# Weights to 32 bits by other operations on three engines, xn on ScalarE, and wider tiles in eight steps

## Chip, cores and metric

The kernel runs on one core of one Trainium2 chip. The time is that of the device, in microseconds (us), for one execution of the whole program. TensorE is called PE, VectorE DVE, ScalarE ACT, GpSimd POOL; SP is the engine whose queue issues the loads and stores.

## The reference

Two parts follow one another. The first is a gated recurrence over 768 steps for 4 batches and 8 heads of 40 (q, k, v, an input gate, a forget gate, an output gate). The second is a normalisation of the 320 columns with a weight g_ln, a layer of 1,280 with a cut at zero, and a second matrix back to 320, added to the input.

```python
for t in range(S):
    m_new = np.maximum(f_gate[:, :, t] + m, i_gate[:, :, t])
    f_stab, i_stab = np.exp(f_gate[:, :, t] + m - m_new), np.exp(i_gate[:, :, t] - m_new)
    C = f_stab * C + i_stab * einsum('bhd,bhe->bhde', vt, kt)
    n = f_stab * n + i_stab * kt
    y[:, :, t] = sigmoid(o_gate[:, :, t]) * (C @ qt) / np.maximum(np.abs(n @ qt), 1.0)
x = y.transpose(0, 2, 1, 3).reshape(B, S, 320)
xn = (x - mu) / np.sqrt(var + 1e-06) * g_ln
out = x + np.maximum(xn @ w_ch1, 0.0) @ w_ch2
```

The two weight matrices arrive as 64-bit floats.

## The kernel before

The 768 steps are cut into 6 chunks of 128, so with 4 batches there are 24 tiles, numbered `st` (chunk 0 is tiles 0 to 3). Two tiles make a pair `p`, and the dense layers run on pairs, 12 of them.

A tile of the recurrence is computed in chunk form. The gates give a table `w` of decay factors, made by a load of a row to all partitions (`G`, line 204), an affine select on POOL (`sel`, line 312) and exponentials on ACT (`ex`, line 323); for tiles 0 to 3 PE makes the argument instead (`gx`, lines 332 and 338). `S` (line 355) is k times q per head, in matmuls of 40 rows whose stationary side has 128 columns for tiles 0 to 3 and two times 64 after that. `P` (line 362) multiplies it by `w` on DVE. `int` (line 391) multiplies the carried state by the scaled q (`qm`, line 368, POOL, with the loaded tile `eg`), again in two halves of 64 columns, and `pv` (line 440) adds the part within the chunk. `kv` (line 406), `sd` and `st` carry the state on. `n1`, `n2` and `n3` (lines 453 to 477) divide, apply the output gate and take the sum of each row on DVE; the last two instructions of `n3` scale that sum to minus the mean (line 475) and write `xn = (y - mean) * g` (line 477). `sq` (line 484) squares and sums on ACT, `np` (lines 490 and 491) makes the inverse deviation `rs` on POOL.

For the dense layers PE transposes xn (`T`, lines 502 and 503); `xh` (ACT, line 509) rounds the result to the matmul's 32-bit format and `xl` (DVE, lines 517 and 520) keeps the residue. `m1` (line 536) does the first matrix in 8 matmuls for each block of 128 of the 1,280 columns: high weight by high x, low by high, high by low. `hh` (ACT, line 541) and `hl` (DVE, line 548) cut at zero and split again; `m2` (lines 563 to 565) does the second matrix in three matmuls per block, `ob` (line 570) adds it to y, scaled by `rs`, and `out` stores it.

The weights come in eleven pieces called keys: 0 is the last 64 rows of the first matrix, the odd keys are 512 columns of its first 256 rows, the even ones 640 columns of the second matrix. A key is loaded as 64-bit words (`wl`, line 587). `cA` (ACT, line 596) takes the absolute value of the high words, `cX` (DVE, line 603) cuts it from below, `cT` (DVE, lines 609, 613 and 617) shifts and masks in three steps, the last writing over the low words. `cH` (ACT, line 638) rounds the result to the high part, `cL` (POOL, line 644) subtracts it and leaves the low part. `cR` copies the pieces of key 0 to the other half of the partitions.

`ORDER` is one list of words written out ahead of the run; a word calls the function of that name, and each engine executes its own instructions in the list's order. Every load and store is issued by SP in that order too, and waits there for its data or its buffer. `fill` (line 681) is a matmul into a bank that nobody reads; 22 of them stand among the first words. The first m1 of the list is that of pair 0, when keys 3, 2, 0 and 1 have been converted. Keys 4 to 10 follow among the dense layers of pairs 0 and 1.

Of the kernel before, what the change touches and what calls it, by code (L numbers as in the profile page):

```python
# [46 lines left out]
gm.3 st.1 st.0 ex.3.1 S.2@4@6 tok.1 P.0.0 cL.1 P.0.1 gta.2@0 cR.0 gtr.1@5 gr.2 gca.2 P.2.1 pv.0 gg.3 n3.1 ld.5 S.3@0@1
cR.2 fill.512 P.2.0 sq.1 sel.5 gtr.2@6 gate.3 fill.513 P.3.1 gex.3 gst.3 gu.3 ex.5.0 gse.3 fill.512 gcr.2 n1.0
fill.512 P.3.0 fill.512 G.4 ex.5.1 n2.0 int.2@0@1 np.1 gta.3@4 ld.4 fill.512 gm.4 int.3@2@3 fill.512 gr.3 gca.3 gg.4
gcr.1 n3.0 gtr.3@6 pv.3 sig.1 pv.2 gcr.3 km.2 sq.0 gate.4 n1.3 gst.4 gex.4 km.3 T.0@4 n2.3 eg.2 T.1@5 n1.2 kv.2@6 gu.4  # L50
xh.0 n2.2 gse.4 xh.1 xl.0 kv.3@2 st.2 S.5@0@3 xl.1 st.3 np.0 gta.4@1 gm.5 sel.4 m1.0.0.0@6 wl.4 gr.4 P.5.0 n3.2
m1.0.0.1 gg.5 ex.4.0 S.4@2@4 wl.5 ex.4.1 P.5.1 gtr.4@5 gca.4 n3.3 hh.0.0 m1.0.1.0@0 qm.5 wl.7 sq.2 T.2@3 m1.0.1.1 qm.4
hl.0.0 sq.3 P.4.0 xh.2 T.3@1 hh.0.1 m2.0.0.1@6 gate.5 np.2 xh.3 gcr.4 gst.5 xl.2 cA.4 m2.0.0.0@7 cR.1 np.3 xl.3 tok.2
gex.5 gu.5 int.4@2@3 gse.5 cX.4 cA.5 cR.3 m1.1.0.0@5 cT.4.0 ld.6 hl.0.1 m1.1.0.1 cT.4.1 m1.1.1.0@1 sd.4 hh.1.0 cT.4.2
m1.1.1.1 hl.1.0 cH.4 P.4.1 gta.5@0 cA.7 m2.1.0.1@5 cL.4 cX.5 hh.1.1 gca.5 cX.7 m2.1.0.0@4 cT.5.0 wl.9 hl.1.1 m2.0.1.1
wl.6 cT.5.1 sig.2 km.4 m2.1.1.1 cT.7.0 km.5 cT.5.2 m2.0.1.0 cT.7.1 cH.5 pv.4 cT.7.2 cL.5 kv.4@0 cH.7 n1.4 m2.1.1.0
# [5 lines left out]
n2.5 ex.6.1 qm.7 n3.5 m2.0.3.0 m2.1.4.1 km.6 ob.1.0 sq.5 kv.6@0 out.1.0 ob.1.1 np.5 S.6@2@3 out.1.1 tok.4 S.8@4@5
P.6.1 P.6.0 m2.0.4.0 T.5@3 ob.0.0 m2.0.3.1 xh.5 out.0.0 xl.5 m2.0.4.1 m1.2.1.0@2 ob.0.1 G.8 m1.2.1.1 out.0.1 G.9
m1.2.4.0@7 ld.9 sig.4 km.9 ld.11 hh.2.1 km.8 m1.2.0.0@3 hl.2.1 m1.2.0.1 m1.2.2.0@6 sel.8 hh.2.0 ld.10 hl.2.0 m1.2.2.1
ex.8.1 eg.4 m1.2.4.1 ex.8.0 P.8.1 sel.9 m2.2.0.0@2 hh.2.2 P.8.0 m2.2.1.0 G.7 hh.2.4 hl.2.2 ex.9.0 m2.2.0.1@3 hl.2.4
ex.9.1 int.6@4@5 pv.6 sd.6 st.6 S.9@6@7 n1.6 n2.6 m1.2.3.0@0 n3.6 m1.2.3.1 qm.9 P.9.1 sq.6 m2.2.1.1 P.9.0 np.6
m2.2.2.1 hh.2.3 sel.7 hl.2.3 S.11@4@5 ex.7.0 S.7@6@7 m2.2.2.0 ex.7.1 P.7.0 T.6@0 m2.2.3.0 P.7.1 xh.6 xl.6 int.7@6@7
pv.7 sd.7 qm.8 st.7 kv.8@0 n1.7 m2.2.3.1 n2.7 n3.7 m2.2.4.1 int.8@6@7 ob.2.1 sq.7 T.7@1 sd.8 pv.8 out.2.1 st.8 np.7
xh.7 G.12 kv.9@3 xl.7 m2.2.4.0 n1.8 n2.8 m1.3.1.0@0 ob.2.0 n3.8 out.2.0 m1.3.3.0@1 m1.3.1.1 ld.15 sq.8 ld.12 T.8@6
sel.12 G.11 hh.3.1 m1.3.3.1 tok.5 xh.8 hl.3.1 np.8 ex.12.0 m1.3.0.0@7 xl.8 m1.3.2.0@2 ex.12.1 m1.3.0.1 hh.3.3 hl.3.3  # L70
S.10@0@6 hh.3.0 hl.3.0 m1.3.2.1 m2.3.0.0@1 hh.3.2 sel.11 hl.3.2 m1.3.4.0@7 G.10 ex.11.0 m1.3.4.1 m2.3.0.1@2 ex.11.1
P.11.0 eg.5 m2.3.1.0 ld.13 P.11.1 sig.5 km.10 m2.3.1.1 km.11 m2.3.2.1 hh.3.4 hl.3.4 int.9@4@5 sel.10 pv.9 sd.9 st.9
ex.10.0 kv.11@7 n1.9 m2.3.2.0 qm.11 n2.9 G.15 ex.10.1 n3.9 m2.3.3.1 qm.10 m2.3.4.1 ld.16 P.10.1 sq.9 T.9@3 P.10.0
m2.3.3.0 G.13 np.9 xh.9 ob.3.1 m2.3.4.0 xl.9 out.3.1 tok.6 sel.15 m1.4.0.0@4 ob.3.0 out.3.0 m1.4.0.1 ex.15.1 S.12@5@6
ex.15.0 S.13@0@2 hh.4.0 P.12.0 sel.13 P.12.1 kv.10@3 m1.4.2.0@1 hl.4.0 ld.14 ex.13.0 eg.6 m1.4.1.0@5 ex.13.1 P.13.0
m1.4.2.1 P.13.1 m1.4.1.1 hh.4.2 sig.6 km.13 hl.4.2 m2.4.0.1@6 hh.4.1 km.12 m1.4.3.0@4 hl.4.1 m1.4.3.1 m2.4.1.1 hh.4.3
# [5 lines left out]
ex.14.1 m2.4.4.1 P.14.0 tok.7 ex.16.0 m1.5.4.0@2 ob.4.1 P.14.1 out.4.1 m1.5.2.1 ex.16.1 eg.7 m1.5.4.1 hh.5.2 hl.5.2
m2.5.0.0@7 m2.5.0.1@4 m2.4.4.0 m2.5.1.0 ob.4.0 hh.5.4 km.15 sig.7 out.4.0 hl.5.4 m1.5.3.1 km.14 T.13@6 hh.5.3 m2.5.1.1
xh.13 qm.14 hl.5.3 kv.15@5 xl.13 S.16@0@1 qm.15 m2.5.2.0 P.16.1 ld.18 P.16.0 m1.6.1.0@2 m1.6.1.1 ld.17 m2.5.3.0 hh.6.1
hl.6.1 m2.5.4.0 m2.5.2.1 ob.5.0 out.5.0 m2.5.3.1 G.17 int.15@0@1 kv.14@3 sd.15 eg.8 pv.15 st.15 m2.5.4.1 n1.15 n2.15
m1.6.3.0@6 n3.15 int.14@0@1 sel.17 m1.6.0.0@2 ob.5.1 sq.15 sd.14 out.5.1 st.14 np.15 ex.17.0 m1.6.0.1 ld.21 qm.16
ex.17.1 m1.6.2.0@7 qm.17 hh.6.0 m1.6.2.1 tok.8 hl.6.0 m1.6.3.1 hh.6.2 ld.19 hl.6.2 m1.6.4.0@5 hh.6.3 hl.6.3 m2.6.0.1@4
m2.6.0.0@3 m2.6.1.0 m2.6.2.0 m2.6.1.1 sig.8 km.17 km.16 m2.6.2.1 G.18 m2.6.3.1 pv.14 kv.16@2 n1.14 m2.6.3.0 n2.14
n3.14 m1.6.4.1 sel.18 int.16@6@7 hh.6.4 S.18@0@1 sq.14 sd.16 hl.6.4 ex.18.0 np.14 pv.16 st.16 kv.17@5 ex.18.1 n1.16
T.14@2 P.18.0 m2.6.4.0 xh.14 n2.16 P.18.1 m2.6.4.1 xl.14 T.15@0 int.17@6@7 ob.6.0 xh.15 S.17@1@2 ob.6.1 out.6.0 xl.15  # L90
G.21 S.21@3@4 out.6.1 sd.17 eg.9 n3.16 m1.7.2.0@0 ld.20 m1.7.2.1 P.17.1 sq.16 eg.10 P.17.0 m1.7.3.0@2 np.16 hh.7.2
# [654 lines left out]
```

## Time and profile before

| what | value |
|---|---|
| median of 3 runs | 350.67 us (350.58 to 353.99) |
| profiled execution | 352.78 us, its span 351.0 us |
| mean granted clock of PE | 0.966 of full |
| moved by DMA | 49.37 MB, mean 141 GB/s |

The profile is of one execution. The span runs from its first to its last recorded instruction; the execution's own time lies a little above it. Busy time of an engine counts its instructions, not its waiting for others. A row of a group gives the line of the kernel, the engine, the operation, the tiles written and read, the shapes and the count, and, behind the bar, the time that the engine was idle ahead of those instructions and what ended it.

### The profile page before, as it was taken

How to read it: one execution, taken by the hardware profiler on the slowest of the kernel's cores; microseconds unless marked ns; L12 is line 12 of the kernel's file. 1: busy time of each engine (PE TensorE's matmuls, PEld its weight loads, DVE VectorE, ACT ScalarE, POOL GpSimd, SP SyncE). 2: the span in 40 equal slices, each digit the busy share in tenths (PEclk: the TensorE clock that was granted, in tenths of full speed). 3: DMA queues.
4: the chain of work that ended last, by engine and by line, in shares of the span. 5: the costliest groups of instructions: out<-in, count | busy, mean ns of one | idle time of the engine just before them, and what ended most of it. 6: DMA issues, size and time to landing. Idle time of an engine off the chain costs nothing.

```text
span 351.0 us, 11943 instructions
## 1 busy us (share of the span) xinstructions
PE 329.6 (94%) x5189; PEld 305.2 (87%) x5189; DVE 208.5 (59%) x486; ACT 145.5 (41%) x374; POOL 116.1 (33%) x158
## 2 busy tenths in 40 slices
PE   7979999997999699899989989999979999999996
PEld 3558688996899699799989979989979999999995
DVE  6775999998636373864955444286454353383232
ACT  3963673454354336562227214145612932142020
POOL 4476683437421531622322224114331201210000
PEclk9965899999999999999999998999998999999999
DMA  8858379890487059692502358029305803010001
GB/s 235 296 145 216 125 243 251 238 311 12 156 228 185 3 150 304 159 291 47 205 36 67 118 152 266 5 103 254 115 4 169 325 2 88 4 39 1 21 19 40
DMA packets 15953, 49.37 MB, mean 141 GB/s; under 512 B 1916, under 2 KB 5532, under 8 KB 15900
## 3 DMA queue, kind: packets, MB, share of 16 engines
q1 hardware_dynamic: 15900, 48.60, 46.3%
q8 instruction: 41, 0.67, 0.8%
q14 instruction: 12, 0.10, 0.1%
HBM read 43.84 MB, written 4.10 MB: 137 GB/s over the span
## 4 chain that ended last, share of the span: by engine, by line
PE 72%; DVE 16%; issue 4%; DMA 4%; ACT 1%; SPq 1%; POOL 1%; DVEq 0%; POOLq 0%
PE banks L536 25%; PE banks L563 9%; PE banks L565 8%; PE banks L564 8%; PE banks L355 6%; PE banks L440 5%; DMA eg<-esc 3%; PE banks L391 3%; DVE wt L613 3%; DVE wraw L617 2%; PE banks L406 2%; PE banks L338 1%; PE banks L681 1%; PE banks L502 1%; DVE wt L603 1%
## 5 line engine op out<-in xcount | busy, mean ns | idle before, releaser
L563 PE MATMUL banks<-w2h,hh 128*128 128x320 f32 x240 | 77.5, 323 | 0.1
L565 PE MATMUL banks<-w2h,hl 128*128 128x320 f32 x240 | 74.9, 312 | 2.1 <-DVE hl L548 1.3
L564 PE MATMUL banks<-w2l,hh 128*128 128x320 f32 x240 | 74.9, 312 | 1.0 <-issue 1.0
L548 DVE SCALAR_TENSOR_TENSOR hl<-banks,hh 128x512 fp32r<-128x512 f32 x60 | 41.1, 689 | 56.0 <-ACT hh L541 55.8
L541 ACT ACTIVATE hh<-banks 128x512 fp32r<-128x512 f32 x60 | 35.5, 595 | 83.4 <-PE banks L536 76.4
L536 PE MATMUL banks<-xh,w1h 128*128 128x256 f32 x360 | 64.8, 289 | 0.0
L536 PE MATMUL banks<-xh,w1l 128*128 128x256 f32 x360 | 63.1, 285 | 0.0
L323 ACT ACTIVATE w<-w,ar_sb 128x128 f32<-128x128 f32 x160 | 48.7, 389 | 14.6 <-POOL w L312 14.5
L536 PEld LDWEIGHTS banks<-xh,w1h 128*128 128x128 f32 x360 | 52.9, 192 | 0.8 <-issue 0.3
L536 PEld LDWEIGHTS banks<-xh,w1l 128*128 128x128 f32 x360 | 51.9, 191 | 0.0
L536 PE MATMUL banks<-xl,w1h 128*128 128x256 f32 x240 | 48.7, 285 | 0.1
L565 PEld LDWEIGHTS banks<-w2h,hl 128*128 128x128 f32 x240 | 45.5, 190 | 2.8 <-DVE hl L548 1.6
L563 PEld LDWEIGHTS banks<-w2h,hh 128*128 128x128 f32 x240 | 45.5, 190 | 2.6 <-issue 1.6
L362 DVE TENSOR_TENSOR w<-banks,w 128x512 f32<-128x512 f32 x48 | 32.2, 686 | 25.2 <-ACT w L323 14.3
L564 PEld LDWEIGHTS banks<-w2l,hh 128*128 128x128 f32 x240 | 45.6, 190 | 0.4 <-POOL w2l L644 0.4
L368 POOL TENSOR_TENSOR qe<-qk,eg 104x512 f32<-104x512 f32 x20 | 26.8, 1354 | 43.6 <-DMA eg<-esc 29.2
L536 PEld LDWEIGHTS banks<-xl,w1h 128*128 128x128 f32 x240 | 37.3, 191 | 0.3 <-issue 0.3
L312 POOL TENSOR_SCALAR_AFFINE_SELECT w<-w 128x1024 f32<-128x1024 f32 x20 | 21.9, 1097 | 46.6 <-DMA w<-gsc 34.2
L484 ACT ACTIVATE junk<-y,sum 128x320 bf16<-128x320 f32 x24 | 13.4, 560 | 50.6 <-DVE sum L475 50.6
L355 PE MATMUL banks<-qk 40*64 40x128 f32 (+1 forms) x704 | 28.2, 285 | 0.0
L355 PEld LDWEIGHTS banks<-qk 40*64 40x64 f32 (+1 forms) x704 | 23.5, 147 | 2.4 <-issue 0.8
L490 POOL TENSOR_SCALAR rs<-rs 128x1 f32<-128x1 f32 x24 | 5.1, 211 | 53.0 <-ACT junk L484 52.0
(85 smaller groups left out, 421.0 us busy)
## 6 DMA issues: line engine op xcount, KB each, us to landing
tok<-in_tok_dram SPq DMA_DIRECT2D x12, 968.0 KB
w<-gsc SPq DMA_DIRECT2D x20, 512.0 KB
qk<-in_qk_dram SPq DMA_DIRECT2D x24, 416.0 KB
out_dram<-y SPq DMA_DIRECT2D x24, 160.0 KB
wraw<-in_w_dram SPq DMA_DIRECT2D x5, 640.0 KB
wraw<-in_w1a_dram SPq DMA_DIRECT2D x5, 512.0 KB
eg<-esc SPq DMA_DIRECT2D x10, 256.0 KB
eg<-esc SPq DMA_DIRECT2D x10, 160.0 KB
```

The costliest lines, as they stand in the source:

```text
L312: nc.gpsimd.affine_select(out=w, in_=w, pattern=[[0, H], [1, C]], compare_op=ALU.is_ge, fill=NEG, base=0, channel_multiplier=-1)
L323: nc.scalar.activation(out=w[:, h], in_=ps[:, hh], func=AF.Exp, bias=ar_sb[:, c, 0, b * H + h:b * H + h + 1])
L355: nc.tensor.matmul(s_t[st, z][m, g], t[r, 1, g, m], t[r, 0, g], start=True, stop=True, skip_group_check=True)
L362: nc.vector.tensor_tensor(out=w, in0=s_t.pop((st, half)), in1=w, op=ALU.mult)
L368: nc.gpsimd.tensor_tensor(out=t, in0=qk_t[st][:, 0], in1=eg_t[p][:, j], op=ALU.mult)
L440: nc.tensor.matmul(Y[m, h], w[:, h, m], tok_t[p][:, j, h * VA:(h + 1) * VA], start=(c == 0), stop=(c == 0 or g == 3), skip_group_check=True,)
L536: nc.tensor.matmul(ps[:, i], a, x, start=(n == 0), stop=(n == len(ops) - 1))
L541: nc.scalar.activation(out=t, in_=h1_t[p, f], func=AF.Relu)
L548: nc.vector.scalar_tensor_tensor(out=l.rearrange("p a t -> p (a t)"), in0=ps.rearrange("p a t -> p (a t)"), scalar=0.0, in1=t.rearrange("p ...
L563: nc.tensor.matmul(ps, t[:, i, sl], w2h[:, ff], start=(ff == 0), stop=False)
L564: nc.tensor.matmul(ps, t[:, i, sl], w2l[:, ff], start=False, stop=False)
L565: nc.tensor.matmul(ps, l[:, i, sl], w2h[:, ff], start=False, stop=(ff == KF - 1))
```

## The change

Each key is converted by other operations. The high words, read as 32-bit floats, are multiplied by 2^-112 on ACT. The top three bits of the low words are made by a multiplication and an addition on 32-bit unsigned words, for even keys on POOL, for odd keys on ACT. DVE then has two operations: shift left by three and join, and join the sign. The high part is made as before, but scaled by g_ln/-320 for the first matrix (two instructions for an odd key). The low part is made on DVE for nine keys (multiply and subtract); for keys 1 and 3 PE forms it in PSUM, the weight times a diagonal of the scale minus the high part, and ACT copies it out.

As g_ln is in the weights, xn needs none: `nx` on ACT writes sum - 320 y. The squares and the deviation take the factor 320 into account. Tiles 10, 11, 14, 15, 18, 19, 22 and 23 use 128 columns at once in `S` and `int`. The fillers read the identity in place of a zeroed tile, there are 20 short and 3 long ones in place of 18 and 4, and `ORDER` is a new list of 1,168 words for 1,151.

```diff
-CX = "ddddddddddd"
-CL = "ppppppppppp"
-BUFS = {'y': 7, 'xt': 2, 'ht': 4, 'wraw': 4, 'w': 5, 'qk': 5}
+CX = "papapapapap"
+CL = "dededdddddd"
+WIDE = (10, 11, 14, 15, 18, 19, 22, 23)
+BUFS = {'y': 7, 'xt': 2, 'ht': 4, 'wraw': 4, 'w': 5, 'qk': 5, 'wt': 3}
...
-int.1@0@1 ini id g0 int.0@2@3 gin wl.3 wl.2 fill.513 gm.0 gg.0 ld.1 gate.0 wl.0 gu.0 gx.1@4@5 wl.1 gm.1 cA.3 gg.1 cX.3
-gta.0@6 fill.512 cT.3.0 fill.512 gr.0 gca.0 cT.3.1 gtr.0@6 ex.1.0 fill.512 fill.512 fill.512 gcr.0 gate.1 cT.3.2
...
+int.1@0@1 ini id cst int.0@2@3 g0 wl.0 fill.513 gin g8 gm.0 gg.0 fill.512 ld.0 gate.0 gu.0 gx.0@4@5 cA.0 cB.0 tok.0
+gm.1 gta.0@6 fill.512 wl.3 fill.512 gr.0 gca.0 ex.0.0 gtr.0@6 fill.512 gcr.0 gg.1 fill.512 cT.0.0 fill.512 ex.0.1
+gx.1@4@6 fill.513 gate.1 ex.1.0 cT.0.1 gu.1 gst.1 fill.512 ld.1 gex.1 S.0@4@5 ex.1.1 gse.1 wl.2 fill.512 ld.2 sig.0
...
-        n = C if st < NE else 64
+        n = C if st < NE or st in WIDE else 64
...
+            n = C if st in WIDE else 64
             for g in range(4):
-                for j in range(2):
+                for j in range(0, C, n):
                     for z in range(2):
-                        r, m = slice(64 * z, 64 * z + D), slice(64 * j, 64 * j + 64)
+                        r, m = slice(64 * z, 64 * z + D), slice(j, j + n)
...
-        nc.vector.tensor_scalar(out=sm, in0=sm, scalar1=-1.0 / DM, scalar2=None, op0=ALU.mult)
+        mu_t[st] = sm
+
+    @piece
+    def nx(st):
         xn = xn_p.tile([128, DM], F32, tag="xn", name="xn")
-        nc.vector.scalar_tensor_tensor(out=xn, in0=y_t[st], scalar=sm, in1=g_sb, op0=ALU.add, op1=ALU.mult)
+        nc.scalar.activation(out=xn, in_=y_t[st], func=AF.Identity, scale=-float(DM), bias=mu_t[st])
...
-        nc.scalar.activation(out=t.bitcast(F32), in_=hi.bitcast(F32), func=AF.Abs)
+        nc.scalar.activation(out=t.bitcast(F32), in_=hi.bitcast(F32), func=AF.Copy, scale=TINY)
...
+    def cB(n):
+        lo = w_st[n][0]
+        if CX[n] == "p":
+            nc.gpsimd.tensor_scalar(
+                out=lo, in0=lo.bitcast(U32), scalar1=TOP3, scalar2=TOP3_B, op0=ALU.mult, op1=ALU.add
+            )
+        else:
+            nc.scalar.activation(out=lo, in_=lo.bitcast(U32), func=AF.Identity, scale=TOP3, bias=t3_sb)
...
         if i == 0:
-            nc.vector.tensor_scalar(
-                out=t, in0=t, scalar1=3, scalar2=0x3FFFFFF8, op0=ALU.logical_shift_left, op1=ALU.bitwise_and
-            )
-        elif i == 1:
             nc.vector.scalar_tensor_tensor(
-                out=t, in0=hi, scalar=-0x40000000, in1=t, op0=ALU.bitwise_and, op1=ALU.bitwise_or
+                out=t, in0=t, scalar=3, in1=lo, op0=ALU.logical_shift_left, op1=ALU.bitwise_or
             )
         else:
             nc.vector.scalar_tensor_tensor(
-                out=lo, in0=lo, scalar=29, in1=t, op0=ALU.logical_shift_right, op1=ALU.bitwise_or
+                out=t, in0=hi, scalar=-0x80000000, in1=t, op0=ALU.bitwise_and, op1=ALU.bitwise_or
             )
...
+        for t, h, _, g in parts(n):
+            nc.scalar.activation(out=h, in_=t, func=AF.Copy, scale=g)
+
+    @piece
+    def cI(n, *at):
...
+        if m == 512:
+            cs = slice(256 * key[1], 256 * key[1] + 256)
+            ops = [(dg_sb[:, k], w1h[:, k, cs], 256 * k, 256 * k + 256) for k in range(2)]
...
+        for d, h, a, z in ops:
+            nc.tensor.matmul(ps[:, a:z], d, w_st[n][:, a:z], start=True, stop=False, skip_group_check=True)
+            nc.tensor.matmul(ps[:, a:z], ni_sb, h, start=False, stop=True, skip_group_check=True)
...
-            e.tensor_tensor(out=l, in0=t, in1=h.bitcast(F32), op=ALU.subtract)
+        if CL[n] == "e":
...
+            nc.scalar.activation(out=l, in_=ps.rearrange("p (k c) -> p k c", k=2), func=AF.Copy)
+        else:
+            for t, h, l, g in parts(n):
+                nc.vector.scalar_tensor_tensor(
+                    out=l, in0=t, scalar=g, in1=h.bitcast(F32), op0=ALU.mult, op1=ALU.subtract
+                )
...
+    def g8():
+        nc.gpsimd.tensor_scalar(out=g_sb, in0=g_sb, scalar1=-1.0 / DM, scalar2=None, op0=ALU.mult)
+        for k in range(2):
+            nc.gpsimd.tensor_scalar(out=dg_sb[:, k], in0=id_sb, scalar1=g_sb[:, k:k + 1], scalar2=None, op0=ALU.mult)
```

## Rows read from the trace of the kernel before

**Rows 1.** The page: busy us of each engine, share of the span, instructions.

```profile
PE 329.6 (94%) x5189; PEld 305.2 (87%) x5189; DVE 208.5 (59%) x486; ACT 145.5 (41%) x374; POOL 116.1 (33%) x158
```

**Rows 2.** Windows: us, busy us of each engine (count), clock, DMA share, GB/s.

```profile
0.00:44.00 44.00, 39.32 (x396) 27.01 (x400) 32.10 (x81) 25.07 (x70) 26.73 (x48) 0.81 0.70 204
...
20.00:35.00 15.00, 14.83 (x165) 12.84 (x165) 8.92 (x23) 7.27 (x22) 9.65 (x13) 0.50 0.67 175
...
44.00:84.00 40.00, 37.68 (x428) 35.30 (x420) 38.33 (x72) 20.89 (x42) 20.49 (x23) 1.00 0.74 230
84.00:100.00 16.00, 13.71 (x323) 13.09 (x324) 10.00 (x23) 6.40 (x17) 8.61 (x9) 1.00 0.41 138
100.00:351.00 251.00, 238.92 (x4052) 229.75 (x4050) 128.03 (x312) 93.17 (x246) 60.24 (x79) 0.99 0.39 116
```

**Rows 3.** Waits of PE over the whole span: us in total, times, longest.

```profile
PE banks L391 <- DVE w L362: 2.6, 2, 1.8
PE banks L332 <- DVE w L362: 2.4, 1, 2.4
PE banks L391 <- issue: 2.3, 2, 1.5
...
PE banks L406 <- issue: 1.9, 1, 1.9
```

**Rows 4.** Timeline, 11 to 22 us: start, length, instruction [idle before <-releaser].

```profile
11.45 1.02 PE L681 MATMUL banks<-wu_sb,id_sb 128*128 128x512 f32 x2
...
15.89 1.16 PE L355 MATMUL banks<-qk 40*128 40x128 f32 x16
...
16.60 2.23 POOL L644 TENSOR_TENSOR w2l<-wraw,w2h 128x640 fp32r<-128x640 f32 x1 [0.41 <-ACT w2h L638]
...
17.43 2.08 DVE L617 SCALAR_TENSOR_TENSOR wraw<-wraw,wt 128x640 int32<-128x640 int32 x1
...
20.17 1.01 PE L332 MATMUL banks<-mk_bf,id_bf 128*128 128x512 bf16 x2 [2.36 <-DVE w L362]
```

**Rows 5.** Windows of the instructions on tile wt alone: DVE, then ACT busy.

```profile
0.00:44.00 44.00, 12.21 (x16) 3.11 (x4) 0.81 0.70 204
44.00:84.00 40.00, 21.94 (x28) 5.12 (x7) 1.00 0.74 230
```

**Rows 6.** Groups by line and shape: count, busy us, mean ns, idle before.

```profile
L541 ACT ACTIVATE hh<-banks 128x512 fp32r<-128x512 f32 x60 | 35.5, 595 | 83.4 <-PE banks L536 76.4 <-PE banks L564 3.6 <-issue 3.1
...
L312 POOL TENSOR_SCALAR_AFFINE_SELECT w<-w 128x1024 f32<-128x1024 f32 x20 | 21.9, 1097 | 46.6 <-DMA w<-gsc 34.2 <-DVE xn L477 12.4
...
L477 DVE SCALAR_TENSOR_TENSOR xn<-y,sum,g_sb 128x320 f32<-128x320 f32 x24 | 18.1, 756 | 1.2 <-DVE sum L475 0.3
...
L484 ACT ACTIVATE junk<-y,sum 128x320 bf16<-128x320 f32 x24 | 13.4, 560 | 50.6 <-DVE sum L475 50.6
...
L475 DVE TENSOR_SCALAR sum<-sum 128x1 f32<-128x1 f32 x24 | 3.7, 153 | 0.8
...
L596 ACT ACTIVATE wt<-wraw 128x512 f32<-128x512 f32 x5 | 3.5, 691 | 3.4 <-DMA wraw<-in_w1a_dram 3.4
L613 DVE SCALAR_TENSOR_TENSOR wt<-wraw,wt 128x512 int32<-128x512 int32 x5 | 3.4, 684 | 0.1
...
L245 POOL TENSOR_SCALAR gg<-gg 32x128 f32<-32x128 f32 x5 | 2.9, 583 | 0.4
```

**Rows 7.** Timeline of PE, 42 to 54 us: tiles at full clock.

```profile
42.10 1.16 PE L406 MATMUL banks<-tok,kp 128*64 128x41 f32 x32
43.19 1.10 PE L355 MATMUL banks<-qk 40*64 40x128 f32 x32
...
44.30 0.64 PE L536 MATMUL banks<-xh,w1h 128*128 128x256 f32 x3
...
52.94 0.68 PE L391 MATMUL banks<-state,qe 40*64 40x41 f32 x32
```

**Rows 8.** The chain that ended last, 101 to 114 us: start, us, what.

```profile
101.72 12.05 DMA eg<-esc
```

More of the change, by code (lines that the diff above doesn't have):

```diff
@@ L47 @@
[L47 to L56, printed above, removed]
@@ L62 @@
[L62 to L71, printed above, removed]
@@ L72 @@
[L72 to L76, printed above, removed]
@@ L82 @@
[L82 to L86, printed above, removed]
@@ L87 @@
[L87 to L91, printed above, removed]
@@ new lines @@
+m1.1.4.0@6 cL.6 ex.8.0 m1.1.4.1 hl.0.3 ex.8.1 cT.8.1 m1.0.4.1 cB.10 cA.10 m2.0.2.0 cH.8 m2.1.2.1 cT.10.0 m2.0.2.1 cL.8
+T.4@7 cT.10.1 hh.1.4 m2.1.2.0 km.7 sig.3 hl.1.4 m2.1.3.0 xh.4 km.6 cH.10 xl.4 m2.0.3.1 qm.6 hh.0.4 cL.10 m2.0.3.0
+int.5@6@7 hl.0.4 pv.5 qm.7 sd.5 kv.6@2 m2.1.3.1 n1.5 ld.8 st.5 m2.1.4.0 n2.5 n3.5 gta.5@1 m2.1.4.1 gca.5 ob.1.0 nx.5
+m2.0.4.0 ob.1.1 sq.5 out.1.0 out.1.1 m2.0.4.1 np.5 ob.0.0 out.0.0 T.5@6 ob.0.1 S.8@1@7 eg.4 xh.5 xl.5 out.0.1
+int.6@3@4 G.9 pv.6 P.8.1 ld.9 sd.6 m1.2.1.0@5 P.8.0 tok.4 st.6 G.7 m1.2.1.1 n1.6 n2.6 G.10 n3.6 ld.10 kv.7@0 qm.8
@@ new lines @@
+P.18.0 m2.7.1.1 P.19.1 m2.7.2.1 P.19.0 m2.7.1.0 m2.7.2.0 S.22@6@7 int.18@3@4 pv.18 sd.18 st.18 m2.7.3.1 n1.18 n2.18
+T.17@2 n3.18 m2.7.4.1 xh.17 xl.17 sq.18 m2.7.3.0 G.20 nx.18 np.18 ob.7.1 m1.8.2.0@3 out.7.1 m1.8.0.0@4 G.22 m2.7.4.0
+m1.8.0.1 ob.7.0 tok.10 eg.10 m1.8.3.0@2 sel.20 hh.8.0 out.7.0 hl.8.0 m1.8.3.1 ex.20.1 m1.8.2.1 ex.20.0 sel.22
+m1.8.1.0@0 hh.8.2 hh.8.3 m1.8.1.1 hl.8.2 ex.22.1 hl.8.3 int.19@3@4 ex.22.0 m2.8.0.1@1 P.22.1 sd.19 hh.8.1 st.19
+m2.8.0.0@2 P.22.0 sig.10 m1.8.4.0@7 hl.8.1 qm.20 m2.8.1.0 m1.8.4.1 qm.21 m2.8.1.1 hh.8.4 hl.8.4 pv.19 S.20@5@6 n1.19
@@ new lines @@
+n2.19 S.21@0@7 n3.19 m2.8.2.1 P.20.0 sq.19 P.20.1 nx.19 np.19 m2.8.2.0 G.21 m2.8.3.0 m2.8.4.0 T.18@3 ob.8.0 T.19@4
+m2.8.3.1 xh.18 out.8.0 xh.19 xl.18 tok.11 int.20@5@6 xl.19 sel.21 int.21@2@3 G.23 m2.8.4.1 ex.21.1 m1.9.1.0@4 ld.23
+ob.8.1 ex.21.0 out.8.1 P.21.1 m1.9.2.0@1 eg.11 P.21.0 m1.9.1.1 m1.9.0.0@7 hh.9.1 hl.9.1 m1.9.0.1 sig.11 m1.9.3.0@0
+hh.9.0 hl.9.0 m1.9.3.1 sel.23 m1.9.4.0@4 hh.9.3 ex.23.0 hl.9.3 m1.9.2.1 ex.23.1 S.23@0@7 hh.9.2 pv.21 P.23.0 qm.22
+pv.20 P.23.1 m1.9.4.1 hl.9.2 qm.23 n1.20 n1.21 m2.9.0.1@0 n2.20 n2.21 m2.9.0.0@7 n3.20 m2.9.1.0 n3.21 nx.20 sq.20
@@ L587, in wl @@
         nc.sync.dma_start(out=t[:, :m], in_=src)
-        w_st[n] = t
+        raw = t[:, :m].bitcast(I32).rearrange("p (n two) -> p n two", two=2)
+        w_st[n] = raw[:, :, 0], raw[:, :, 1]
     @piece
@@ L678, in fill @@
     @piece
-    def fill(n):
-        a, x = (id_sb, wu_sb) if n > 512 else (id_bf, wu_sb.bitcast(BF16)[:, :n])
-        nc.tensor.matmul(banks[:, 7, 0:x.shape[1]], a, x, start=not busy, stop=False, skip_group_check=True)
+    def g8():
+        nc.gpsimd.tensor_scalar(out=g_sb, in0=g_sb, scalar1=-1.0 / DM, scalar2=None, op0=ALU.mult)
+        for k in range(2):
+            nc.gpsimd.tensor_scalar(out=dg_sb[:, k], in0=id_sb, scalar1=g_sb[:, k:k + 1], scalar2=None, op0=ALU.mult)
+    @piece
+    def fill(n):
+        a = id_sb if n > 512 else id_bf
+        x = a.unsqueeze(1).to_broadcast([128, 4, 128])
+        nc.tensor.matmul(
+            banks[:, 7].rearrange("p (a b) -> p a b", a=4), a, x, start=not busy, stop=False, skip_group_check=True
+        )
         busy.append(n)
```

153 lines of the change are left out of this document (91 added, 62 removed).

## The prediction

> **What bounds the kernel now.** I read the page first: PE is busy 94% of the span, DVE 59%, ACT 41%, POOL 33% [rows 1]. So the question is which microseconds are not PE at full clock, and the windows split them [rows 2]. From 100 us on PE is busy 238.92 of 251.00: that stage is PE's, and 12.1 us with the tail after the last matmul is all there is to win. From 44 to 84 DVE is busy 38.33 of 40, which looks like the bound, but PE is busy 37.68 of the same 40 at full clock: a faster DVE finds only 2.3 us of PE idle there, and 2.3 more from 84 to 100. Before 44 it is different: PE is idle 4.7, part of its 396 matmuls are fillers, and for the 15 us from 20 on its clock is 0.50, the lower level.
>
> The waits of PE say what the idle ends on [rows 3]: the DVE product w (2.6 late and 2.4 early) and issue, which no engine causes (2.3 and 1.9). The timeline shows how the early one comes about [rows 4]: POOL's residue of weights runs from 16.60 to 18.83, a DVE weight operation that starts beside it at 17.43 lasts 2.08 and ends 0.68 after it, the products w are queued behind that, and PE stands 2.36 and then runs at half clock.
>
> **The change, part by part.** The sum is made on the profiled execution, 352.78 us (span 351.0). The median of the runs is 350.67, so 2.1 comes off at the end.
>
> *DVE up to 44 us.* Four keys cost DVE 12.21 in 16 operations [rows 5]. After, a key has two operations of 0.684 at 512 columns [rows 6], so 0.855 at 640. Keys 3 and 1 leave their residue to ACT: 1.37 each. Key 2 adds a residue of 0.855: 2.57. Key 0 has two on 64 partitions: 3.42. That is 8.7, or 3.5 less. The scaled mean and xn of two tiles go too, 0.153 and 0.756 each [rows 6], 1.8: 5.3 less of 32.1 busy. DVE is idle 11.9 in this stage, so some of it only lengthens waits. Ends: nothing, and 12 (the 4.7 idle and 7.5, what half clock costs in 15 us). I take 5: the 2.4 gap, as the POOL residue that blocked it is gone, and a third of the 7.5, as the new order starts with tiles 0 and 1 and has thin places of its own. Three f32 fillers for four and 20 bf16 for 18 change nothing.
>
> *DVE from 44 to 100.* Seven keys cost 21.94 in 28 operations [rows 5]. After: six operations of 0.684 and eight of 0.855 (10.9), residues of 0.684 for three keys and 0.855 for four (5.5), and 1.6 of blocking as a guess: 18.0, so 3.9 less, and three xn with their means 2.7 less. PE has 4.6 idle in these two windows to answer with [rows 2]. Ends 0 and 4.6; I take 3.
>
> *ACT.* It gains 24 xn at 0.560 (the square of the same tile is the row), five low words at 0.691 (as the high words of 512 columns), two residues at 0.595 [rows 6], and the halves of five first-weight keys become two instructions, some 0.3 more each by estimate. Up to the last key that is five xn, 2.8, and 3.5, 1.2 and 1.5: 9.0. ACT is busy 46.0 of the first 84 us [rows 2]; 38 of idle cover it. I take nothing; without that cover it is rival three.
>
> *POOL.* Its eleven residues go, and six low words come. Their price is not in the trace: low end 1.10, the affine select of 1,024 columns; high end 2.9, five times the 0.583 of 128 columns [rows 6]. I take 1.1, the row with 128 partitions and one input. The three small products for the diagonal and the negative identity run while POOL waits for the gates. Nothing on the path.
>
> *Differences on PE.* Two keys get an f32 pass over 512 columns, 1.02 [rows 4], and two f32r passes over 256, under 0.43 (0.64 for three) [rows 7]: 1.4 each. The first falls among fillers, the second stands right before the first m1. Ends 0 and 2.9; I take 1.4.
>
> *Wider tiles.* S takes 1.16 in 16 wide matmuls [rows 4] and 1.10 in 32 narrow ones [rows 7]: nothing. The narrow int takes 0.68 in 32 [rows 7]; a wide one is in no row. If the number of instructions sets it, it is 0.3 less; if it goes as S does, 0.4 more; nearest is kv of 64 columns, 1.16 for two tiles, 0.58 each. Eight steps: ends -2.4 and +3.2; I take 0.
>
> *SP.* The table of g goes ahead of the gates, for which the first scan on DVE waits: one issue, +0.5. The reordered loads (tok ahead of weights, raw buffers free one step sooner as the result now lies in wt) move traffic that I have no row to price: 0.
>
> *After 100 us.* 19 xn and means, 17.3 of 128.03, leave DVE; T now waits for ACT after the sum. That adds a wait to ACT's queue where the square already has it. The late wait on w, 2.6, ends a chain that starts with 12.05 of loading the eg tile [rows 8]; the new order issues that load ahead of the three qk loads that now precede it. The 4.2 of issue stay. Ends 0 and 9 (12.1 without a tail of some 3); I take 4, the 2.6 and 1.4 of shorter waits. Next late is PE itself.
>
> Sum: -5 - 3 + 1.4 + 0 + 0.5 - 4 = -10.1. So 342.7 for such an execution and **340.6** against the median.
>
> **A rule that speaks against it.** In the trace a DVE operation of two tiles in memory lasted as long as the POOL one beside it, then its own 0.68 [rows 4]; the change keeps 22 such and adds the residues. The Trainium skill (SBUF — State Buffer, Who interferes with whom) says that a DVE instruction with two SBUF inputs contends with a GpSimd one that reads SBUF, and the later fully blocks. The trace agrees (2.08 against 0.855 by columns); by the rule alone each POOL low word, too, would be added to DVE, which is rival two.
>
> **The rivals.** *One: the clock stays full.* If the early gap has no successor, the first part gives 12, not 5: 335.7, so 333.6. For it: one gap of 2.36 stands ahead of the whole half-clock stretch. Against it: between tiles 0 and 1 PE has little but fillers.
>
> *Two: POOL goes on blocking DVE.* Six low words of 1.1 to 2.9 are 6.6 to 17.4 us in which DVE's two-input operations stand; the 5.3 and 6.6 taken off DVE are eaten, and both early terms are zero: -2.1, so 348.6, no difference. For it: the 2.08. Against: eleven residues of up to 2.23 are gone from the same place. That PE was full there anyway gives the same number.
>
> *Three: ACT's queue becomes the bound, and it is slower.* ACT works in order; low words, split halves and xn stand ahead of hh and of the exponentials, each waiting for DVE or a load. If its 38 us of idle are waits that stay, the 9.0 lie on the path up to the last key and the early terms are zero: -2.1 + 9.0, so 357.6. It is slower by over 1% once 5.6 of the 9.0 find no idle. For it: ACT waited 50.6 for the mean, where xn now stands too. Against: 76.4 of its idle is waiting for PE ahead of hh, which is cover [rows 6].
>
> **How the numbers follow.** Forecast 0.54, rival one 0.20, two 0.14, three 0.12. A measurement of this kernel tells about 1% from no change: below 347.2 is faster, above 354.2 slower. Forecast and rival one are faster, 0.74; two is the same, 0.14; three is slower, 0.12. With every gain at its end (12, 4.6, 9 and 2.4 off, 0.5 on) the time is 323; rival three is 357.6. With one in ten left out at each side the range is 329 to 352.
>
> **What would show it.** Right: DVE busy some 12 us less in the first 84; a shorter stretch at the lower clock; the first m1 at about 39 instead of 44.30 [rows 7]; int of a wide step near 0.6. Wrong: low words on POOL above 2 us; DVE operations of 0.855 still lasting 2; hh late behind ACT's new work; a second stretch at the lower clock, or longer gaps of issue.

## The result, and the profile after

The changed kernel takes 337.50 us (median of 4 runs) where the kernel before takes 350.62 (4 runs): ratio 0.962, 95% interval 0.953 to 0.972. The forecast was 340.6. Timed again on the chip of the last experiments it took 337.07 against 349.28, ratio 0.966 (0.961 to 0.971). Ratios leave out executions that lie well above the kernel's fastest, and as the first profiled one of the changed kernel was such (346.76 us; what was different in it is told in the last section), the rows below are of a repetition of 336.29 us, span 334.5.

The page (busy us of each engine, share of the span, instructions) answers to [rows 1]:

```profile
PE 321.7 (96%) x4945; PEld 300.4 (90%) x4945; DVE 181.9 (54%) x429; ACT 159.4 (48%) x410; POOL 108.1 (32%) x156
```

DVE has lost 26.6 us, ACT has gained 13.9, PE has 244 matmuls fewer. The windows answer to [rows 2], in the same columns; the last two lines cut at the first m1:

```profile
0.00:44.00 44.00, 38.81 (x508) 27.54 (x508) 33.51 (x85) 34.73 (x95) 27.48 (x53) 1.00 0.83 248
20.00:35.00 15.00, 13.75 (x214) 10.51 (x212) 13.41 (x34) 13.28 (x39) 9.82 (x15) 1.00 0.75 247
44.00:84.00 40.00, 39.41 (x558) 38.16 (x551) 34.90 (x65) 25.13 (x57) 20.30 (x24) 1.00 0.62 197
84.00:100.00 16.00, 14.62 (x282) 13.50 (x280) 6.95 (x17) 6.71 (x17) 4.80 (x7) 1.00 0.87 253
...
0.00:37.33 37.33, 32.68 (x411) 21.80 (x411) 27.60 (x73) 28.41 (x78) 23.02 (x44) 1.00 0.81 247
37.33:334.50 297.17, 289.01 (x4538) 278.57 (x4534) 154.30 (x357) 131.01 (x333) 85.06 (x112) 1.00 0.45 134
```

The kernel before, cut at its own first m1:

```profile
0.00:44.30 44.30, 39.62 (x401) 27.14 (x402) 32.39 (x82) 25.07 (x70) 27.03 (x48) 0.81 0.70 204
44.30:351.00 306.70, 290.02 (x4789) 278.01 (x4789) 176.07 (x405) 120.46 (x304) 89.05 (x111) 0.99 0.44 131
```

These four lines are the account. Up to the first m1 the gain is 6.97 us. PE's busy time there fell by 6.94 (39.62 to 32.68), and its idle time stayed what it was (4.68 and 4.65). Most of this gain is the lower clock, 0.50 from 20 to 35 us before [rows 2] and 1.00 now; in the trace's own record of the clock the stretch at 0.50 runs from 20.11 to 37.17. By an estimate from the same matmuls in the two timelines (16 small matmuls of `gx` keep PE for 2.0 us there and for 1.1 here) that stretch cost 6.8 us. Some 2.0 more come from a slower start, which differs between executions of one kernel (last section), so they are no merit of the change. Against both stand 1.3 us of matmuls more, the 2.4 of the residues less one long filler and smaller things. That makes 7.5 for the 6.94 measured. After the first m1 it is the other way round: 9.53 us are gained, of which PE's busy time gives 1.0 and its idle time 8.5 (16.7 to 8.2). The two profiles stand 16.5 apart, the medians of the last series 12.2, since the profile of before was of a longer execution than its median.

PE's waits, which answer to [rows 3] (us in total, times, longest):

```profile
PE banks L725 <- POOL id_sb L694: 1.7, 1, 1.7
PE banks L286 <- ACT state L433: 1.3, 1, 1.3
PE banks L573 <- ACT hh L551: 1.2, 1, 1.2
PE banks L345 <- DVE gc L259: 1.2, 1, 1.2
PE banks L448 <- issue: 1.2, 1, 1.2
PE banks L546 <- issue: 0.9, 1, 0.9
...
PE banks L414 <- issue: 0.2, 1, 0.2
```

Three lines of the kernel before that [rows 3] leaves out belong beside them:

```profile
PE banks L391 <- DVE xh L520: 2.1, 1, 2.1
...
PE banks L564 <- issue: 1.0, 2, 0.7
PE banks L565 <- issue: 0.8, 1, 0.8
```

The waits on w, 2.6 and 2.4, are gone, and so is the one on xh. Ahead of the first m1 two others, on `gc` and on the copy of the state, have taken the place of the early one, and no stretch at the lower clock follows them. The waits called issue, 6.0 before over all lines, are 2.3.

The stretch of [rows 4], 18 to 22 us (start, length, instruction):

```profile
18.35 0.68 DVE L627 SCALAR_TENSOR_TENSOR wt<-wraw,wt 128x512 int32<-128x512 int32 x1
18.40 1.26 POOL L613 TENSOR_SCALAR wraw<-wraw 128x640 int32<-128x640 uint32 x1 [0.83 <-DMA wraw<-in_w_dram]
...
19.48 1.16 PE L362 MATMUL banks<-qk 40*128 40x128 f32 x16
20.57 0.70 PE L663 MATMUL banks<-wt,dg_sb 128*128 128x256 f32 x2
20.92 0.47 PE L664 MATMUL banks<-w1h,ni_sb 128*128 128x256 f32 x1
21.23 0.60 PE L663 MATMUL banks<-wt,dg_sb 128*128 128x256 f32 x2
21.48 0.47 PE L664 MATMUL banks<-w1h,ni_sb 128*128 128x256 f32 x1
21.79 0.60 PE L339 MATMUL banks<-mk_bf,id_bf 128*128 128x512 bf16 x2
```

DVE's operation came 0.05 ahead of POOL's low word and was not lengthened; POOL's took 1.26, where the shortest of its six takes 0.78. PE forms the residue of key 3 from 20.57 to 21.79. The matmuls of the line at which it stood 2.36 us before (L332 then, for tile 3; L339 now, for tile 2) follow without a wait.

Groups (count, busy us, mean ns, idle before), the prices that [rows 6] had to bound:

```profile
L488 ACT ACTIVATE xn<-y,sum 128x320 f32<-128x320 f32 x24 | 13.3, 554 | 30.2 <-DVE y L480 30.2
...
L613 POOL TENSOR_SCALAR wraw<-wraw 128x640 int32<-128x640 uint32 x6 | 6.7, 1112 | 8.6 <-DMA wraw<-in_w_dram 5.2 <-DMA wraw<-in_w1r_dram 1.6 <-DVE state L435 0.9
L623 DVE SCALAR_TENSOR_TENSOR wt<-wt,wraw 128x640 int32<-128x640 int32 x6 | 6.0, 994 | 1.0 <-POOL kp L383 1.0
L678 DVE SCALAR_TENSOR_TENSOR w2l<-wt,w2h 128x640 fp32r<-128x640 f32 x5 | 5.9, 1181 | 0.4 <-ACT w2h L649 0.4
...
L617 ACT ACTIVATE wraw<-wraw,t_sb 128x512 int32<-128x512 uint32 x5 | 3.8, 764 | 1.1 <-DMA wraw<-in_w1a_dram 1.1
...
L399 PE MATMUL banks<-state,qe 40*128 40x41 f32 x128 | 8.3, 279 | 0.0
L399 PE MATMUL banks<-state,qe 40*64 40x41 f32 x384 | 7.8, 228 | 0.0
```

### The profile page after: what moved, and what is told of

Read it like the earlier page. It is cut to its first block, busy times and chain, and to the rows that moved or that the text cites. A ratio compares the mean times of both kernels' runs of the same rounds, so it can differ in the third digit from the quotient of the medians.

```text
span 344.9 us, 11420 instructions
## 1 busy us (share of the span) xinstructions
PE 333.9 (97%) x4945; PEld 307.7 (89%) x4945; DVE 181.9 (53%) x429; ACT 159.2 (46%) x410; POOL 106.2 (31%) x156
## 4 chain that ended last, share of the span: by engine, by line
PE 81%; DMA 6%; DVE 5%; issue 2%; ACT 2%; POOL 1%; SPq 0%; DVEq 0%; POOLq 0%; ACTq 0%
PE banks L546 27%; PE banks L573 11%; PE banks L575 10%; PE banks L574 10%; PE banks L362 6%; PE banks L448 5%; PE banks L399 4%; DMA wraw<-in_w1a_dram 3%; PE banks L725 2%; PE banks L345 2%; PE banks L414 2%; DMA w<-gsc 2%; PE banks L512 1%; ACT w L330 1%; DVE wt L623 1%
## 5 line engine op out<-in xcount | busy, mean ns | idle before, releaser
L574 PE MATMUL banks<-w2l,hh 128*128 128x320 f32 x240 | 74.1, 309 | 0.0
L546 PE MATMUL banks<-xh,w1h 128*128 128x256 f32 x360 | 63.8, 286 | 0.2 <-DVE hl L558 0.2
L546 PE MATMUL banks<-xh,w1l 128*128 128x256 f32 x360 | 62.4, 282 | 0.0
L546 PEld LDWEIGHTS banks<-xh,w1h 128*128 128x128 f32 x360 | 51.7, 188 | 1.3 <-issue 0.5
L546 PEld LDWEIGHTS banks<-xh,w1l 128*128 128x128 f32 x360 | 51.2, 189 | 0.0
L369 DVE TENSOR_TENSOR w<-banks,w 128x512 f32<-128x512 f32 x48 | 31.5, 683 | 23.1 <-PE banks L362 16.4
L488 ACT ACTIVATE xn<-y,sum 128x320 f32<-128x320 f32 x24 | 13.3, 554 | 30.2 <-DVE y L480 30.2
L500 POOL TENSOR_SCALAR rs<-rs 128x1 f32<-128x1 f32 x24 | 5.8, 243 | 64.3 <-ACT junk L494 63.6
```

Source lines behind the costliest of these rows:

```text
L369: nc.vector.tensor_tensor(out=w, in0=s_t.pop((st, half)), in1=w, op=ALU.mult)
L546: nc.tensor.matmul(ps[:, i], a, x, start=(n == 0), stop=(n == len(ops) - 1))
L574: nc.tensor.matmul(ps, t[:, i, sl], w2l[:, ff], start=False, stop=False)
```

## The experiments

The theory after the result: the operations and the list of words are worth little apart and 13 us together, because only together do they leave no gap in the first 25 us after which PE's clock falls. The rivals: one of them does it alone; a moved single step (xn, the residue on PE, the wide tiles) does it.

**The change in two halves.** First the whole once more, as a baseline beside them:

> The changed kernel once more, for a ratio over more rounds and for further profiles. Both theories: 335 to 339, ratio 0.96. In the first profile PE ran S of tile 0 in 2.08 instead of 1.16 and kept that pace up to 33 us. If that pace differs between executions of this one kernel, a profile whose time is about 337 will show the full pace before 20 us (S of tile 0 in about 1.1) and the first m1 some 8 us earlier than the other (about 38 against 46). If it is a part of the change itself, the slow pace to 33 us is there again.

Measured 337.19, ratio 0.963 (0.957 to 0.968), first m1 at 37.11. Then the operations alone. In the list, `cB` makes the low words, `cX` and `cT` are DVE's steps on a key, `cI` is the residue on PE, `cst` and `g8` load and prepare the table of g:

```diff
-ORDER = (the new list)
+ORDER = (the list of before, with cB for cX, no third cT, nx after n3, cst and g8 at the start)
-CL = "dededdddddd"
+CL = "ddddddddddd"
-WIDE = (10, 11, 14, 15, 18, 19, 22, 23)
+WIDE = ()
```

> The new operations put into the old list: weights, xn on ACT, g in the weights, nx directly behind n3, no wide tiles, all residues on DVE, nothing on PE for them. Theory one (the operations give the early gain, as DVE is relieved): about 343 (5 + 3 off, 1 of the late 4, 0.5 on). Theory two (the new list gives it): 349 to 352. Theory three (ACT's queue becomes the bound when the list isn't made for it): over 354.

Measured 345.97, ratio 0.989 (0.984 to 0.995). And the list alone:

```diff
-ORDER = (the list of before)
+ORDER = (the new list, with cX and three cT for cB and two, no cI, g8 and WIDE; xn on DVE where nx stands)
```

> The old operations put into the new list: old weight operations, residues on POOL, xn on DVE with g at the place of nx, no matmuls for residues, no wide tiles, table of g loaded after the first gates. Theory one: the early DVE work is back to old size, so 348 or more, and DVE is busy over 36 of 40 us between 44 and 84. Theory two: 337 to 341.

Measured 352.26, ratio 1.000 (0.995 to 1.006). So 1.1% and nothing, where both together give 3.7%: the product of the two ratios, 0.990, leaves 9 us unexplained by either. The profiles, one of each, say where the two need each other. The first m1 comes at 45.35 with the operations alone and at 45.48 with the list alone, later than the 44.30 of before, and at 37.33 with both (39.2 to 39.8 where PE reached full pace as late as in the profile of before; last section). Behind it the operations gain 4.3 and the list 2.4, where both gain 9.5. Neither half has the residues on PE nor the wide tiles, which are tried further down. PE's timeline, operations alone (an execution of 349.69 us, 3.7 above the median):

```profile
16.67 0.82 PE L725 MATMUL banks<-id_bf 128*128 128x512 bf16 x3
19.14 1.01 PE L339 MATMUL banks<-mk_bf,id_bf 128*128 128x512 bf16 x2 [1.65 <-DVE w L369]
20.09 2.08 PE L345 MATMUL banks<-gc,id_sb 32*128 32x128 f32 x16
```

and the list alone:

```profile
22.85 1.16 PE L356 MATMUL banks<-qk 40*128 40x128 f32 x16 [2.57 <-DVE y L463]
24.79 1.01 PE L333 MATMUL banks<-mk_bf,id_bf 128*128 128x512 bf16 x2 [0.78 <-DVE w L363]
25.73 2.08 PE L339 MATMUL banks<-gc,id_sb 32*128 32x128 f32 x16
```

In each, PE stands for DVE, and 16 small matmuls, which take 1.16 at full clock, take 2.08 soon after. The windows of the two (the line of 20 to 35 us, then for the second 44 to 84) show how far it reaches. Operations alone:

```profile
20.00:35.00 15.00, 13.94 (x163) 12.71 (x162) 10.71 (x21) 7.49 (x25) 4.38 (x10) 0.50 0.64 177
```

List alone:

```profile
20.00:35.00 15.00, 11.66 (x105) 9.13 (x103) 11.18 (x29) 8.12 (x24) 6.78 (x12) 0.65 0.80 247
...
44.00:84.00 40.00, 33.46 (x461) 30.93 (x459) 38.17 (x72) 21.14 (x52) 23.52 (x28) 0.98 0.80 235
```

The old list leaves its gap at the wait on w, 1.65 us long instead of 2.36, and the clock of 0.50 is there again in this execution; the other five had a mean clock of 0.980 to 0.990 where it had 0.959, so theirs was lower for a shorter time. With the new list and the old operations PE waits 2.57 us for DVE early, and from 44 to 84 it has 33.46 of 40 busy beside a DVE of 38.17.

**The clock by itself.** Fillers (matmuls that nobody reads) ahead of those that wait on w, with nothing else changed, should bring back what the lower clock costs. In the kernel before:

```diff
+fill.512 (10 times, ahead of gx.3@4@5)
```

> The kernel before with ten more short fillers ahead of the argument matmuls of tile 3, where PE waited 2.36. Clock theory (the early gain is that no early gap is long enough to bring the lower clock): the stretch at 0.50 goes or shrinks, the first m1 comes 2 to 6 us before 44.30, the time falls by 2 to 6 us, to 345 to 348. Rival (DVE's work is the bound up to the first m1, the clock only fills its waits): the stretch goes, the first m1 stays within 1 us of 44, the time within 1 us of 350.4.

Measured 350.32, ratio 0.996 (0.990 to 1.002). In its profile (351.52 us) the gap of 2.36 went and the clock held to 32.4 us, but two gaps of 1.4 and 1.5 behind POOL's and ACT's work on the gates came there and the clock fell. The first m1 came at 42.53, 1.8 earlier. One of its twelve executions had a mean clock of 1.00, and it took 343.98, the fastest of them; the others had 0.961 to 0.985 and took 347.27 to 353.30. In the operations alone, with the same fillers:

```diff
+fill.512 (8 times, ahead of gx.3@4@5)
+fill.512 (4 times, ahead of pv.0)
```

> The new operations in the old list (346.0) with eight more short fillers ahead of the argument matmuls of tile 3 and four ahead of the pv of tile 0, the places of its waits of 1.65 and 1.06. Clock theory: the stretch at 0.50 goes, first m1 from 45.35 to 39 to 41, time 340 to 342. Rival (the new list's order of the loads and tiles gives the rest): the first m1 within 1.5 us of 45, the time 345 to 347.

In its profile (352.61 us) the clock is 1.00 up to 84 us and the first m1 comes at 40.80 instead of 45.35: the step from the gap to the clock to the first m1 holds, 4.5 us of it. But the median is 352.09 (ratio 0.994, 0.988 to 0.999), no better than without them. From the first m1 on the profiled execution takes 310.0 us, against 302.4. PE's waits of this run:

```profile
PE banks L415 <- issue: 6.1, 4, 2.0
PE banks L575 <- issue: 3.9, 2, 2.0
PE banks L514 <- issue: 2.1, 1, 2.1
```

12.1 us of issue, 6.7 without the fillers, and the clock below 1.00 again in places behind them (0.89 from 84 to 100 us). So the theory was right on its first half and wrong on the whole: an earlier first m1 is not kept by itself. What these waits are is shown below.

**Single steps.** xn on DVE again, at the new list's place:

```diff
-nc.scalar.activation(out=xn, in_=y_t[st], func=AF.Identity, scale=-float(DM), bias=mu_t[st])
+nc.vector.scalar_tensor_tensor(out=xn, in0=y_t[st], scalar=-float(DM), in1=mu_t[st].to_broadcast([128, DM]), op0=ALU.mult, op1=ALU.add)
```

> The changed kernel with xn on DVE again, at the place of nx (0.55 to 0.76 each, the mean not scaled). If xn on ACT was worth what I put to it (2.7 - 0.5 early, some 1.4 late): 339 to 341. Rival: PE is full and covers it in either place: 337.

Measured 340.51, ratio 0.968 (0.959 to 0.977): 0 to 3 us, not told apart from the whole change, which was not timed beside it. The residues of keys 1 and 3 on DVE, without PE's matmuls:

```diff
-CL = "dededdddddd"
+CL = "ddddddddddd"
-cI.3@6, cI.1@6
```

> The changed kernel with the residues of keys 1 and 3 on DVE and no matmuls for them. My sum charged 1.4 for the matmuls on the path: 336 if DVE has room for the two residues (0.95 each) there, and the first m1 at 36. Rival: DVE is the one that is short before the first m1, or PE falls idle where the matmuls stood and the clock falls: 338 or more.

Median 343.10, from 336.32 to 354.69, a spread too wide to place it. Its profile is of 342.14 us. PE's timeline where the residue of key 3 was formed, and the window behind it:

```profile
23.25 0.59 PE L339 MATMUL banks<-mk_bf,id_bf 128*128 128x512 bf16 x2 [0.78 <-DVE w L369]
```

```profile
20.00:35.00 15.00, 13.83 (x146) 11.04 (x143) 11.30 (x25) 10.47 (x30) 7.45 (x14) 0.65 0.67 227
```

Without the 1.2 us of matmuls PE stands 0.78 for w, and the clock falls again: 0.65 in this window, first m1 at 42.6. What the prediction charged as a cost of 1.4 was cover in this execution. It is not always needed: two of the six, 336.32 and 338.17, are as fast as the whole change, with a mean clock of 0.993 and 1.00. Whether it is the cover or the work off DVE that counts was asked with fillers in place of the matmuls:

```diff
-cI.3@6
+fill.512 fill.512 fill.512 fill.512 fill.512
-cI.1@6
+fill.512 fill.512 fill.512 fill.512 fill.512
```

> The changed kernel with the residues of keys 1 and 3 on VectorE, and five short fillers (some 1.07 us at full clock) in each place where TensorE formed them. Theory (the residue's matmuls matter as cover: they keep TensorE busy while VectorE finishes w): no gap of 0.4 or more ahead of the exponent matmuls near 23 us, granted clock 1.00 from 20 to 35 us, first m1 at 38 to 40 us, time 335 to 339. Rival (it matters that the residue is off VectorE): the gap or a VectorE wait comes back elsewhere, first m1 at 42 or later, time 341 to 344 as without fillers.

Median 345.95 (337.08 to 347.08), neither the one theory's number nor the other's. In its profile (346.41 us) PE ran at the lower pace from its start until some 33 us, so the first five fillers themselves took 2.32 and the clock had nothing to lose. The first profile of the whole change, with the same slow start, took 346.76, and the one execution of 337.08 equals that change's median. Like is equal to like, which speaks for cover, but one execution does not settle it; it stays open.

**The wide tiles.** The change without them:

```diff
-WIDE = (10, 11, 14, 15, 18, 19, 22, 23)
+WIDE = ()
```

> The changed kernel with all S and int from tile 4 on in halves of 64 columns. My sum had 0 for the wide steps: 337, ratio to the changed kernel 1.00. If fewer instructions save issue, 2 to 3 more: 340. If wide int costs 0.4 a step, 3 less: 334.

Measured 334.77, ratio 0.955 (0.949 to 0.961), beside 337.19 for the whole change. That looked like 2.4 us, so both ran again side by side:

> The changed kernel once more, for a comparison with the next kernel on the same chip. Theory (the wide tiles cost time): this one is the slower of the two by 2 to 4 us; a wide step of int shows 16 matmuls in about 1.02 us. Rival (they cost nothing, the difference seen before was spread): the two are within 1 us.

> The changed kernel with no wide tiles. Theory: 333 to 336 us, 2 to 4 less than the changed kernel in the same call; int takes about 0.61 us for 32 narrow matmuls in all later tiles. Rival: within 1 us of it.

337.07 and 337.49: within 1 us, as the rival said, and the 2.4 did not come again. The groups show that int did get dearer: eight wide steps of it take 8.3 us (above), 1.04 each, where a narrow one takes 0.65 (12.9 in 20, below); all of int is 3.2 us more and S 0.4. The narrow kernel's group of int, and two windows of it:

```profile
L399 PE MATMUL banks<-state,qe 40*64 40x41 f32 x640 | 12.9, 228 | 0.2 <-DVE w L369 0.2
```

```profile
136.00:140.00 4.00, 1.88 (x136) 1.53 (x132) 3.00 (x7) 2.62 (x7) 2.00 (x2) 1.00 0.48 137
140.00:144.00 4.00, 3.91 (x39) 3.85 (x39) 1.33 (x5) 1.10 (x3) 1.46 (x3) 0.58 0.02 4
```

In this execution the narrow kernel stood for issue 0.65 and 1.36 at 138 to 140 us and ran at 0.58 of the clock for the 4 us behind it. That gave back 4 times 0.42, 1.7 us, and its waits for issue were 0.9 longer in all than the whole change's. Its first m1 came at 39.22, 1.9 later than the 37.33, although the two kernels are the same up to there; that is the start again (last section). These are 4.5 against the 3.6 saved, where its profile is 1.6 us longer: 0.7 is not accounted for. No version tried is measurably better than the change. But the fastest executions of the narrow kernel, 332.14 and 332.75 in its two series, lie 2 to 3 us below those of the whole change, 335.29 and 335.07, so a gain of that size is not excluded.

**The waits called issue.** In all these profiles most of them begin at nearly the same numbers of PE records, matmuls and weight loads together, whatever matmul stands there. PE records so far at each wait of 0.2 us or more after 80 us (length of the wait):

```
before            1957 (0.77) 3989 (0.70) 5264 (0.82) 6281 (1.52) 7047 (0.33) 8317 (1.93)
before + fillers  2718 (1.10) 3989 (2.73) 5264 (1.45) 5519 (1.34) 7047 (1.20) 8317 (1.45)
operations        1957 (0.88) 2717 (0.56) 5261 (1.61) 6278 (1.50) 7044 (0.67) 8314 (1.51)
operations + f.   1957 (2.02) 2718 (1.96) 3988 (1.90) 5261 (2.12) 5516 (1.54) 7044 (1.26) 8314 (1.25)
whole change      3739 (0.88) 8826 (1.17)
narrow            3739 (0.61) 4103 (0.65) 4247 (1.36) 9848 (0.27)
```

Read across the kernels, the steps from one such number to the next are multiples of 253.3 to 255.5 (1957 to 2718 is 3 times 253.7, 5264 to 6281 is 4 times 254.3, 8826 to 9848 is 4 times 255.5); only 4103 stands off the row. In the eight profiles not listed four more do, at 3983, 4003 and twice 4007, and all others after 80 us stand on it; the five off it are alike in line (L448) and length (0.46 to 0.65). To test it, 64 tiny matmuls were put in where PE waits for its first loads:

```diff
+if n == 8:
+    for _ in range(64):
+        nc.tensor.matmul(banks[:, 7, :8], id_bf, id_bf[:, :8], start=not busy, stop=False, skip_group_check=True)
```

> The changed kernel with no wide tiles and, after the start, 64 matmuls of 8 columns into the fillers' bank: nothing but 128 more recorded TensorE instructions (64 matmuls, 64 weight loads) in a stretch where TensorE waits for loads. Theory (the waits called issue are waits for the next block of 256 instructions): those over 0.9 us again begin where the number of TensorE records so far is 0.4 to 0.7 above a multiple of 256, so at other matmuls of the program than without the 64; the time is within 1% of the narrow kernel's. Rival (they belong to certain matmuls, after a semaphore or a change of shape): they stay at the same matmuls, 0.9 to 1.2 above a multiple of 256.

Measured 337.58, ratio 0.968 (0.963 to 0.972), as the narrow kernel. None of its waits reaches 0.9 us. The ones after 80 us stand at 5775 (0.83), 9338 (0.32) and 9848 (0.22): the first is 5264 plus twice 255.5, the second 8826 plus twice 256, and the last is the count at which the narrow kernel waited too, though 128 records earlier in the program. The narrow kernel's wait (start, length, instruction):

```profile
296.04 0.39 PE L546 MATMUL banks<-xh,w1l 128*128 128x256 f32 x1 [0.27 <-issue]
```

and that of the shifted one, at the same count and another matmul:

```profile
293.07 0.71 PE L448 MATMUL banks<-tok,w 128*32 128x41 f32 x51 [0.22 <-issue]
```

One early wait of 0.25 kept its matmul and moved from 137 to 265 records, so that one belongs to the program. For those on the row the count decides, and the traces hold the cause. The profile lists a DMA queue of its own for instructions, whose packets are timed. At each wait on the row, in all 14 profiles, PE goes on 1.2 to 1.6 us after one of these packets has landed: before, packets land at 87.45, 146.41, 176.67, 208.72, 229.34 and 260.44, and PE resumes at 88.85, 147.87, 178.04, 210.02, 230.72 and 261.86. The waits off the row end 5 to 11 us after one, so they are no waits for instructions. How many of these points turn into a wait goes with the list: the four profiles with the old list wait 6.1 to 12.1 us there, the ten with the new list 0.2 to 3.1, the old operations in it among them (2.0).

## Why the prediction was right, and where it was not

The forecast's sum was -10.1 on the profiled execution and 340.6 against the median; 337.5 was measured, faster, inside the range. On the profiles it is -7.0 up to the first m1, where the steps -5, +1.4 and +0.5 make -3.1, and -9.5 behind it, where -3 and -4 make -7. By its steps:

- *DVE up to 44 us, -5.* Measured -7.0 at the first m1, which came at 37.33, not at about 39. The term was 2.4 for the gap and 2.5 for a third of the half clock. The gap's 2.4 did not come: idle time ahead of the first m1 is 4.65 for 4.68, as waits on gc and on the state took its place. The half clock came whole: 6.8 by the estimate above, where the step took 2.5, and the row that it read ended at 35 us, two before the stretch did. The other 2.0 are the start of this execution. From starts nearer to that of before (10.78 to 11.40 us for 9.87) the same list without wide tiles, which come later, has its first m1 at 39.22 to 39.75, 4.5 to 5.1 earlier than before. So the step's mechanism was right, both its sizes were off in opposite directions, and that 5 and 39 come so near is in part luck. Rival one had the condition right (the clock stays full) and was 4 us too low; it counted the 4.7 of idle time as well, which stayed.
- *DVE from 44 to 100, -3.* PE's busy time in the two windows rose by 1.73 and 0.91, 2.6 together. DVE's weight operations came out dearer than taken where they met POOL: the first operation of an even key took 0.994 in the mean and the residue 1.181, where 0.855 was taken and 1.6 for all blocking.
- *ACT and xn, 0.* xn took 0.554 for the 0.560 taken, the low word 0.764 for 0.691. PE waited 1.2 for hh: rival three named the place, with 1.2 of its 9.0.
- *POOL, 0.* The low word took 1.11 in the mean for the 1.1 taken, the longest 2.15. Rival two's lock is there, but short: at 18.40 POOL was the one to wait, and the waiting of DVE that the means above show is 1.1 us for the first operation (6.0 less six times 0.81, its undisturbed length) and 1.9 for the residue (5.9 less five times 0.81), both over all even keys, and the second operation of an odd key has 1.3 more (1.37 and 1.30 at two keys, where 0.68 is undisturbed). That is the behaviour that the Trainium skill (SBUF — State Buffer, Who interferes with whom) states, the later instruction being the one that waits.
- *PE's residue, +1.4.* 1.2 for each of the two keys on PE's timeline, so the price was right. But the first lies inside the gap it fills, and taking it out did not make the profiled execution faster but brought the lower clock back. The sign of this term was wrong there; in the two executions without it that were as fast as the whole change, neither sign shows.
- *Wide tiles, 0.* int took the upper end: 0.4 more a step, 3.2 in eight. The medians showed none of it; in the profile the narrow kernel lost as much to its start, to issue and to a short stretch at the lower clock.
- *SP, +0.5.* The first scan on DVE began at 4.25 for 2.83, 1.4 later (at 3.48, 0.65 later, in the profile of 346.76 us), and PE's wait for gc behind it grew from 0.2 to 1.2. The term was too small by up to 0.9.
- *After 100 us, -4, with the 4.2 of issue left where they are.* The step whose reason failed. From the first m1 on 9.5 us were gained where the sum has 7 for both later terms. The late waits on w and xh went, 4.7 together, which covers the 4 that was taken; issue went from 6.0 to 2.3. The step knew 4.2 of it and left that where it was. That part came with the new list, which the prediction looked at for DVE's sake alone.

The windows did not show DVE 12 us less busy in the first 84, since by then the changed kernel is 7 us further on: 68.4 for 70.4. The whole span shows it, 26.6 less.
